# An S4 convolution gated by a feed-forward branch on Trainium2: the gate written back into PSUM, the kernel sums of two channel sets in one visit, and a new order of the projection stage

## The chip, the cores and the metric

The kernel runs on one core of a Trainium2 chip. A core has five engines that run side by side, each with its own queue of instructions which it takes in order: TensorE (PE in the profile, with its weight loads as PEld), VectorE (DVE), ScalarE (ACT), GpSimd (POOL) and SyncE (SP), which here only issues DMA transfers. They wait for one another through semaphores. The metric is the device time of one execution in microseconds (us).

## The reference, cut to what matters

```python
def _A_ref(u, A_re, A_im, B_re, B_im, C_re, C_im, log_dt, Dskip):
    dt = jnp.exp(log_dt)[:, None]
    logdA, dB = dt * (A_re + 1j * A_im), dt * (B_re + 1j * B_im)
    P = jnp.exp(logdA[:, :, None] * l[None, None, :])
    K = jnp.einsum("dn,dnl,dn->dl", Cc, P, dB).real
    ...  # y = causal convolution of u with K, by FFT
    return y + u * Dskip

def _B_ref(x, w1, b1, w2, b2):
    h = _gelu(jnp.einsum("bsd,df->bsf", x, w1) + b1)
    return jnp.einsum("bsf,fd->bsd", h, w2) + b2

x = A_u  # 1 x 2048 x 512
xn = _layernorm(x, axis=-1)
s = _A_ref(xn, ...)  # 128 states per channel
g = _silu(_B_ref(xn, ...))  # 512 -> 1792 -> 512
return x + s * g
```

## The kernel before, in words

The program has two stages. The first, here called the projection stage, does the layer norm, the two projections of branch B, and the convolution kernels K of branch A. The second does the convolution itself as a sequence of small DFT matmuls, multiplies by the gate and adds x. The change edits the first stage only.

*Projections.* The 2,048 rows are cut into four blocks of 512, the 1,792 hidden features into 14 sets of 128. Seven sets' weights are on the chip at a time, so the rows are passed twice: 8 x 7 = 56 steps of one row block and one feature set. Every fp32 operand is split into a rounded part and a rest (h and l at the end of a name), and each product is the sum of three fp32r matmuls. A step goes through five kinds of work. `first_half` (token F, in two halves of 6 matmuls, lines 243 to 252) sums into a PSUM bank with the tag `f1`; there are two such banks. `gate` (G, line 264, ScalarE) adds b1 and applies gelu, from that bank into the SBUF tile `hf`, of which there are two. `gate_high` (H, line 270, ScalarE) rounds `hf` to `hh`, and `ffn_rest` (R, line 276, VectorE) subtracts to get the rest `hl`. `second_part` (S, four pieces of 3 matmuls, lines 289 to 291) sums `hh` and `hl` times w2 into four PSUM banks `z`, over the seven sets. The row transposes of the layer norm (TF) use the `f1` banks too: ScalarE copies them out to `xh`, VectorE subtracts to `xl`.

*Convolution kernels.* The 512 channels are cut into 32 sets of 16. For a set, TensorE computes phases (A, line 593), ScalarE or VectorE rounds them (B), VectorE wraps them (C), ScalarE takes sines (N), GpSimd makes magnitudes (Z), and VectorE multiplies both into the tables e1 and e2 (E, three pieces, lines 642 to 649; two buffers of each table). `gen_sum` (Q, line 657) then sums over the states in 64 small matmuls of a 128 x 32 tile, into one PSUM bank with the tag `sm`; `gen_out` (U) copies the result out on ScalarE and `gen_keep` (UD) sends it to DRAM.

*The order.* The instructions of each engine stand in the order in which the tokens of the string `ORDER` are run; no scheduler moves them. Further tokens: P, steps of the parameters of 128 channels; W, WB and WS, loading and splitting of weights; L with a second letter, the layer norm (LS statistics, LR root, LC scaling); O and ZA to ZD, the z banks' way out. In the names that are shown later, `f_2_3` is row block 2 of the eight passes and feature set 3 of the seven; `kg` is the bank of `gen_sum`, `xT` a transpose, `ra` a set's phases, `w1l` the rest of a weight.

Of the kernel before, what the change touches and what calls it, by code (L numbers as in the profile page):

```python
# [20 lines left out]
P = 128  # L21
# [27 lines left out]
WS.0.3 LD.0 LD.1 P.0 WS.1.0 WS.1.1 P.0 P.0 WS.1.2 G.0 F.1.0 LS.2.0 W.2 LS.3.1 H.0 R.0 WB.2 S.0.0 P.0  # L49
S.0.1 LS.3.0 LL.4 WS.1.3 P.0 WS.2.0 LL.5 W.3 F.1.1 WS.2.1 WB.3 S.0.2 LS.2.1 WS.2.2 G.1 WS.2.3 W.4 S.0.3  # L50
F.2.0 P.0 F.2.1 H.1 WS.3.0 R.1 WS.3.1 P.0 S.1.0 WS.3.2 WB.4 G.2 P.0 WS.4.0 S.1.1 W.5 WS.3.3 P.0 H.2
WS.4.1 P.0 WB.5 F.3.0 P.0 S.1.2 P.0 WS.4.2 LR.2 F.3.1 G.3 S.1.3 R.2 WS.5.0 WS.5.1 KL.0.0 F.4.0 WS.4.3.1
W.6 F.4.1 LC.2 H.3 LC.3 S.2.0 G.4 KL.0.1 TF.2.0 WB.6 BB A.0.0 TH.2.0 LS.5.0 R.3 S.2.1 KL.1.0 TF.2.1
LS.4.0 B.0.0.1 TH.2.1 TL.2.0 C.0.0 WS.6.0 S.2.2 S.2.3 H.4 TF.3.0 A.0.1 KL.1.1 WS.5.2 S.3.0 LS.5.1 WS.6.1
Z.0 B.0.1 P.0 P.1 TH.3.0 S.3.1 C.0.1 S.3.2 A.1.0 N.0.0 TL.2.1 S.3.3 KL.2.0 LD.2 TL.3.0 WS.6.2 B.1.0.1
C.1.0 R.4 F.5.0 TF.3.1 Z.1 LD.3 LS.4.1 N.0.1 A.1.1 B.1.1.1 F.5.1 S.4.0 WS.5.3.1 TH.3.1.1 C.1.1 G.5 S.4.1
E.0.0 S.4.2 S.4.3 E.0.1 TL.3.1 F.6.0 H.5 N.1.0 R.5 F.6.1 LR.4 N.1.1 F.7.0 E.0.2 G.6 A.2.0 B.2.0.1 S.5.0
KL.2.1 LC.5 H.6 F.7.1 S.5.1 P.1 LC.4 C.2.0 WS.6.3 LK.0 F.8.0 S.5.2 A.2.1 G.7 KL.3.0 H.7 B.2.1 P.1 F.8.1
R.6 G.8 KL.3.1 C.2.1 N.2.0 S.5.3 F.9.0 E.1.0 N.2.1 Q.0 A.3.0 S.6.0 S.6.1 S.6.2 F.9.1 Z.2 E.1.1 R.7 U.0
E.1.2 P.1 LD.5 B.3.0.1 LD.4 C.3.0 O.0.0 TF.4.0 KL.4.0 Q.1 Z.3 O.0.1 H.8 S.6.3 TH.4.0 O.0.3 G.9 A.3.1  # L60
S.7.0 TL.4.0 B.3.1.1 P.1 H.9 S.7.1 C.3.1 O.0.2 KL.4.1 TF.4.1 UD.0 LL.6 TH.4.1 R.8 F.10.0 F.10.1 E.2.0
S.7.2 S.7.3 N.3.0 E.2.1 A.4.0 TL.4.1 P.1 S.8.0 R.9 KL.5.0 U.1 E.2.2 N.3.1 B.4.0.1 G.10 OK.0 S.8.1 F.11.0
E.3.0 F.11.1 S.8.2 C.4.0 A.4.1 S.8.3 Q.2 G.11 B.4.1 H.10 UD.1 TF.5.0 E.3.1 E.3.2 LK.1 F.12.0 H.11 TH.5.0
C.4.1 A.5.0 KL.6.0 LS.6.0 F.12.1 B.5.0.1 S.9.0 S.9.1 R.10 N.4.0 G.12 S.9.2 TL.5.0 TF.5.1 P.1 N.4.1 C.5.0
KL.5.1 S.9.3 F.13.0 A.5.1 U.2 TH.5.1 F.13.1 R.11 S.10.0 P.1 B.5.1 Z.4 P.1 P.1 Q.3 C.5.1 N.5.0 TL.5.1
S.10.1 P.1 E.4.0 P.1 UD.2 U.3 F.14.0 N.5.1 H.12 E.4.1 S.10.2 KL.6.1 UD.3 S.10.3 R.12 E.4.2 Z.5 G.13 A.6.0
S.11.0 S.11.1 F.14.1 H.13 LK.2 E.5.0 R.13 E.5.1 LL.7 S.11.2 S.11.3 B.6.0.1 C.6.0 Q.4 Z.6 S.12.0 G.14
A.6.1 KL.7.0 F.15.0 E.5.2 P.1 S.12.1 LS.7.0 B.6.1 LS.7.1 F.15.1 P.2 C.6.1 S.12.2 A.7.0 S.12.3 G.15 LS.6.1
F.16.0 B.7.0 C.7.0 LR.6 N.6.0 A.7.1 S.13.0 LC.6 KL.8.0 S.13.1 U.4 H.14 R.14 P.1 H.15 F.16.1 N.6.1 LC.7
P.2 UD.4 E.6.0 B.7.1 R.15 S.13.2 LD.6 KL.7.1 C.7.1 F.17.0 Z.7 S.13.3 F.17.1 G.16 TF.6.0 O.1.0 O.1.2 Q.5  # L70
A.8.0 E.6.1 G.17 TF.7.0 S.14.0 TH.6.0 P.2 TH.7.0 E.6.2 O.1.1 U.5 O.1.3 H.16 KL.8.1 TL.6.0 TL.7.0 B.8.0
N.7.0 Z.8 S.14.1 S.14.2 N.7.1 S.14.3 F.18.0 OK.1 UD.5 C.8.0 TF.6.1 A.8.1 P.2 Q.6 F.18.1 S.15.0 B.8.1.1
R.16 TH.6.1 S.15.1 C.8.1 S.15.2 U.6 KL.9.0 S.15.3 E.7.0 H.17 E.7.1 S.16.0 W.7 S.16.1 G.18 WB.7 A.9.0
KL.9.1 F.19.0 F.19.1 R.17 E.7.2 B.9.0 TL.6.1 N.8.0 S.16.2 W.8 LD.7 S.16.3 N.8.1 G.19 S.17.0 TF.7.1 C.9.0
A.9.1 E.8.0 P.2 H.18 KL.10.0 TH.7.1 E.8.1 Q.7 B.9.1.1 UD.6 C.9.1 KL.10.1 H.19 D S.17.1 S.17.2 A.10.0
E.8.2 S.17.3 N.9.0 WB.8 F.20.0 TL.7.1 P.2 F.20.1 U.7 KL.11.0 N.9.1 R.18 Z.9 B.10.0 S.18.0 C.10.0 E.9.0
A.10.1 Q.8 G.20 F.21.0 XL.0 W.9 S.18.1 B.10.1 C.10.1 KL.12.0 N.10.0 E.9.1 N.10.1 WB.9 S.18.2 E.9.2 R.19
S.18.3 W.10 F.21.1 A.11.0 F.22.0 U.8 B.11.0 C.11.0 S.19.0 KL.11.1 G.21 H.20 S.19.1 A.11.1 S.19.2 UD.7
Z.10 B.11.1 P.2 P.2 F.22.1 UD.8 LK.3 S.19.3 R.20 F.23.0 WB.10 G.22 C.11.1 E.10.0 N.11.0 S.20.0 Z.11
A.12.0 F.23.1 N.11.1 S.20.1 Q.9 H.21 O.2.0 S.20.2 E.10.1 E.10.2 B.12.0 KL.12.1 F.24.0 H.22 C.12.0 A.12.1  # L80
# [89 lines left out]
def kernel(  # L170
# [1036 lines left out]
```

## Time and profile before

| | before |
|---|---|
| three timed runs | 547.81, 548.02, 549.68 us; median 548.02 |
| the profiled execution | 548.29 us, span on the core 546.5 us |
| mean granted TensorE clock | 0.996 |
| projection stage, by the last large matmul | to about 407 us |
| ScalarE, busy over the span | 394.5 us (72%) |
| VectorE, busy over the span | 463.9 us (85%) |
| GpSimd, busy over the span | 279.1 us (51%) |

Busy times are sums over one execution. Matmuls overlap in the records: each row lasts about 0.4 us where the next starts after 0.235, so TensorE's progress is read from starts, not from durations. A group's row gives the line, engine, operation, tiles (out<-in), shape, count, then the busy time in us and the mean of one in ns, and behind the last bar the time that the engine stood idle ahead of these instructions and who ended it. A row of waits gives who waited for whom, the sum in us, the count and the longest.

### The profile page before, as it was taken

The numbers are of one execution on the slowest core, as the hardware profiler recorded it, in microseconds if no ns is written. First come the engines' busy times: TensorE is split into PE (matmuls) and PEld (weight loads), VectorE is DVE, ScalarE is ACT, GpSimd is POOL, SyncE is SP. The second block draws the span as 40 slices with busy tenths as digits, with TensorE's granted clock in tenths as the row PEclk, the third lists the DMA queues.
The fourth block names the chain that finished last, engine by engine and source line by source line (L and its number), as shares of the span: only waits on it lengthen the run. The fifth ranks groups of instructions, "written<-read, shape, count | busy, mean of one in ns | idle before, by whom it ended". The sixth has DMA issues, their size and how long they took to land.

```text
span 546.5 us, 16626 instructions
## 1 busy us (share of the span) xinstructions
PE 526.9 (96%) x6999; PEld 421.2 (77%) x6999; DVE 463.9 (85%) x736; ACT 394.5 (72%) x570; POOL 279.1 (51%) x385
## 2 busy tenths in 40 slices
PE   8898999999999999999999999999999999999993
PEld 7666787778776777777777777777789998997971
DVE  6899989999999889999888797789557688787896
ACT  3777998898987899959799777889664573652430
POOL 5648379358968559996854296356301001203031
PEclk9999999999999999999999999999999999999998
DMA  8937526744385172837038412913547749361562
GB/s 228 315 124 227 196 83 221 237 150 146 121 245 180 33 237 90 270 102 198 18 110 263 123 47 84 188 45 103 204 160 221 136 127 189 120 194 67 182 208 93
DMA packets 88391, 85.85 MB, mean 157 GB/s; under 512 B 42134, under 2 KB 65050, under 8 KB 87292
## 3 DMA queue, kind: packets, MB, share of 16 engines
q1 hardware_dynamic: 79248, 66.43, 41.6%
q0 software_dynamic: 8768, 17.83, 10.6%
q8 instruction: 55, 0.90, 0.7%
q10 hardware_dynamic: 300, 0.53, 0.3%
q14 instruction: 20, 0.16, 0.1%
HBM read 51.22 MB, written 33.55 MB: 155 GB/s over the span
## 4 chain that ended last, share of the span: by engine, by line
PE 76%; DVE 17%; issue 2%; ACT 1%; POOL 1%; DMA 1%; DVEq 0%; ACTq 0%; POOLq 0%
PE s L913 11%; PE z L289 8%; PE z L290 7%; PE z L291 7%; PE f L250 7%; PE f L252 7%; PE f L251 7%; PE s L891 6%; PE sa L949 6%; PE kg L657 5%; PE ph L593 2%; DVE hl L276 2%; DVE ra L607 2%; DVE e L646 1%; PE y L989 1%
## 5 line engine op out<-in xcount | busy, mean ns | idle before, releaser
L619 POOL TENSOR_TENSOR mm<-mm,rc 128x32 f32<-128x32 f32 (+4 forms) x150 | 115.4, 769 | 11.8
L289 PE MATMUL z<-w2h,hh 128*128 128x512 f32 x224 | 97.8, 437 | 0.0
L250 PE MATMUL f<-xh,w1h 128*128 128x512 f32 x220 | 91.4, 416 | 0.0
L291 PE MATMUL z<-w2h,hl 128*128 128x512 f32 x224 | 88.4, 395 | 0.3 <-DVE hl L276 0.3
L252 PE MATMUL f<-xh,w1l 128*128 128x512 f32 x220 | 87.1, 396 | 1.7 <-DVE w1l L235 1.7
L290 PE MATMUL z<-w2l,hh 128*128 128x512 f32 x224 | 88.6, 395 | 0.0
L251 PE MATMUL f<-xl,w1h 128*128 128x512 f32 x220 | 86.7, 394 | 0.0
L913 PE MATMUL s<-X,mc 64*64 64x128 f32 x1536 | 60.4, 273 | 0.2 <-issue 0.2
L930 DVE TENSOR_TENSOR t<-s,uh 128x512 f32<-128x512 f32 x64 | 41.0, 684 | 22.8 <-ACT uh L921 22.6
L276 DVE TENSOR_TENSOR hl<-hf,hh 128x512 fp32r<-128x512 f32 x56 | 52.9, 948 | 4.6 <-ACT hh L270 4.6
L616 POOL COPY mm<-rc 128x32 f32<-128x32 f32 x30 | 13.4, 446 | 77.7 <-DVE e L649 53.4
L264 ACT ACTIVATE hf<-f,b1s 128x512 f32<-128x512 f32 x56 | 38.2, 688 | 20.4 <-DVE hl L276 11.7
L252 PEld LDWEIGHTS f<-xh,w1l 128*128 128x128 f32 x220 | 41.3, 188 | 12.9 <-DVE w1l L235 3.0
L289 PEld LDWEIGHTS z<-w2h,hh 128*128 128x128 f32 x224 | 42.5, 190 | 10.5 <-issue 1.0
L291 PEld LDWEIGHTS z<-w2h,hl 128*128 128x128 f32 x224 | 42.1, 188 | 10.7 <-DVE hl L276 0.7
L607 DVE SCALAR_TENSOR_TENSOR ra<-ra,ph 128x512 f32<-128x512 f32 x64 | 43.6, 681 | 7.5 <-ACT ra L601 6.5
L913 PEld LDWEIGHTS s<-X,mc 64*64 64x64 f32 x1536 | 44.5, 133 | 5.8 <-issue 1.7
L290 PEld LDWEIGHTS z<-w2l,hh 128*128 128x128 f32 x224 | 42.3, 189 | 8.3 <-DVE w2l L235 0.2
L250 PEld LDWEIGHTS f<-xh,w1h 128*128 128x128 f32 x220 | 41.5, 189 | 9.2 <-ACT hf L264 0.2
L251 PEld LDWEIGHTS f<-xl,w1h 128*128 128x128 f32 x220 | 41.4, 188 | 9.0
L921 ACT COPY uh<-s 128x512 f32<-128x512 f32 x32 | 18.7, 586 | 38.3 <-PE s L913 18.4
L642 DVE TENSOR_TENSOR e<-mm,ra 128x1024 f32<-128x1024 f32 x32 | 42.0, 1311 | 4.7 <-POOL pr_h L524 2.4
(184 smaller groups left out, 1161.1 us busy)
## 6 DMA issues: line engine op xcount, KB each, us to landing
x<-in_A_u_dram SPq DMA_DIRECT2D x8, 512.0 KB
xs<-x SPq DMA_DIRECT2D x8, 512.0 KB
xt_h<-xh POOLq DMA_DIRECT2D x4, 1024.0 KB, 5.5
xt_l<-xl POOLq DMA_DIRECT2D x4, 1024.0 KB, 7.6
kgd<-ko SPq DMA_DIRECT2D x32, 128.0 KB
za<-zo SPq DMA_DIRECT2D x4, 1024.0 KB
xh<-xt_h POOLq DMA_DIRECT2D x4, 1024.0 KB, 6.1
xl<-xt_l POOLq DMA_DIRECT2D x4, 1024.0 KB, 10.1
```

What stands on the lines that cost most here:

```text
L250: PE.matmul(p, wh[:, k, :], xh[:, k, :], start=(k == 0), stop=False)
L251: PE.matmul(p, wh[:, k, :], xl[:, k, :], start=False, stop=False)
L252: PE.matmul(p, wl[:, k, :], xh[:, k, :], start=False, stop=(k == KD - 1))
L276: V.tensor_sub(hl, hf, hh)
L289: PE.matmul(z, hh[:, s], wh, start=(f0 == 0 and not rows), stop=False)
L290: PE.matmul(z, hh[:, s], wl, start=False, stop=False)
L291: PE.matmul(z, hl[:, s], wh, start=False, stop=(f0 == FA - 1))
L607: V.scalar_tensor_tensor(ra[:, 0, c], ra[:, 1, c], MAGIC, p, op0=ALU.subtract, op1=ALU.subtract)
L619: GP.tensor_mul(mv[:, :, 0:3:2, w:2 * w], mv[:, :, 0:3:2, 0:w], rc[:, 2 + 2 * i:4 + 2 * i, :].rearrange("p j c -> p c j").unsqueeze(3).to_ ...
L642: V.tensor_mul(e1, m1.unsqueeze(1).to_broadcast([P, 2, CH, N1]), ra[:, :, :, :N1])
L913: PE.matmul(p[ka * 64:(ka + 1) * 64, r, o, :, jj], w, xf[b][h, c, :, k, :], start=(c == 0), stop=(c == 1), skip_group_check=True)
L930: V.tensor_mul(t, p[:, i, :, 1].unsqueeze(1).to_broadcast([P, 2, 2, P]), uh)
```

## The change

Three things are edited.

1. `gate` writes its result back into the PSUM bank that it reads; `hf` is no tile of its own any more. `gate_high` and `ffn_rest` therefore read the bank, and it is free for new matmuls only when `ffn_rest` has run. `hh` and `hl` get four buffers instead of three.
2. `gen_sum` runs for every second set, over the tables of two neighbouring sets: 128 matmuls into one bank of twice the used width. `gen_out` and `gen_keep` run half as often, on twice the size.
3. `ORDER` is replaced. Besides the places, it says for which halves ScalarE and for which VectorE rounds the phases: VectorE has 31 of the 64 in place of 35.

```diff
 ORDER = """
-WS.0.3 LD.0 LD.1 P.0 WS.1.0 WS.1.1 P.0 P.0 WS.1.2 G.0 F.1.0 LS.2.0 W.2 LS.3.1 H.0 R.0 WB.2 S.0.0 P.0
...
+WS.0.3 P.0 LD.0 P.0 P.0 WS.1.0 WS.1.1 WS.1.2 F.1.0 G.0 H.0 LD.1 W.2 R.0 WS.1.3 F.1.1 WS.2.0 LS.2.0 G.1
...
     def gate(v, f):
-        hf = wka.tile([P, TB * P], F32, tag="hf", name=f"hf_{v}_{f}", bufs=2)
-        A.activation(hf, pt.pop((v, f)), AF.Gelu_apprx_tanh, bias=b1s[:, f:f + 1])
+        hf = pt.pop((v, f))
+        A.activation(hf, hf, AF.Gelu_apprx_tanh, bias=b1s[:, f:f + 1])
         ht[v, f] = hf

     def gate_high(v, f):
         hf = ht[v, f]
-        hh = wka.tile([P, TB * P], F32R, tag="hh", name=f"hh_{v}_{f}", bufs=3)
+        hh = wka.tile([P, TB * P], F32R, tag="hh", name=f"hh_{v}_{f}", bufs=4)
         A.copy(hh, hf)
         ht[v, f] = (hf, hh)

     def ffn_rest(v, f):
         hf, hh = ht[v, f]
-        hl = wka.tile([P, TB * P], F32R, tag="hl", name=f"hl_{v}_{f}", bufs=3)
+        hl = wka.tile([P, TB * P], F32R, tag="hl", name=f"hl_{v}_{f}", bufs=4)
         V.tensor_sub(hl, hf, hh)
         ht[v, f] = (hh, hl)
...
     def gen_sum(s):
-        e1, e2 = gen[s]["e"]
-        p = pss.tile([P, DD, N2], F32, tag="sm", name=f"kg{s}")
-        for d in range(DD):
-            for c in range(2):
-                for g in range(G):
-                    PE.matmul(p[g * N1:(g + 1) * N1, d, :], e1[:, c, g * DD + d, :], e2[:, c, g * DD + d, :],
-                              start=(c == 0), stop=(c == 1), skip_group_check=True)
+        p = pss.tile([P, 2, DD, N2], F32, tag="sm", name=f"kg{s}")
+        for n in range(2):
+            e1, e2 = gen[s - 1 + n]["e"]
+            for d in range(DD):
+                for c in range(2):
+                    for g in range(G):
+                        PE.matmul(p[g * N1:(g + 1) * N1, n, d, :], e1[:, c, g * DD + d, :], e2[:, c, g * DD + d, :],
+                                  start=(c == 0), stop=(c == 1), skip_group_check=True)
         gen[s]["p"] = p

     def gen_out(s):
-        gen[s]["ko"] = ko = par.tile([P, DD, N2], F32, tag="ko", name=f"ko{s}", bufs=2)
+        gen[s]["ko"] = ko = par.tile([P, 2, DD, N2], F32, tag="ko", name=f"ko{s}")
         A.copy(ko, gen[s]["p"])

     def gen_keep(s):
-        b, j = divmod(s, SPB)
-        SY.dma_start(kgd[b][:, j * DD * N2:(j + 1) * DD * N2], gen.pop(s)["ko"].rearrange("p a b -> p (a b)"))
+        b, j = divmod(s // 2, SPB // 2)
+        SY.dma_start(kgd[b][:, j * 2 * DD * N2:(j + 1) * 2 * DD * N2], gen.pop(s)["ko"].rearrange("p n a b -> p (n a b)"))
```

The three places of which the prediction speaks, as the engines' queues have them. First, TensorE at the sums of the first sets (`e_0` and `e_1` are the tables of sets 0 and 1); before:

```order
L252 MATMUL f_1_2_895<-xh_600,w1l_408 128x512
L657 MATMUL kg_907<-e_0_764,e_0_763 32x64 x32
L593 LDWEIGHTS lh_869
L593 MATMUL ph_0_940<-cbs,lh_869 128x512
L289 MATMUL z_0_373<-w2h_640,hh_6_828 128x512
```

and now:

```order
L287 MATMUL z_0_929<-w2h_250,hh_0_860 128x512
L288 MATMUL z_0_929<-w2l_251,hh_0_860 128x512
L289 MATMUL z_0_929<-w2h_250,hl_0_894 128x512
L359 MATMUL xT_0_939<-ident,x_406 128x128 x4
L655 MATMUL kg_962<-e_0_756,e_0_755 32x64 x32
L655 MATMUL kg_962<-e_1_855,e_1_854 32x64 x32
L287 MATMUL z_1_930<-w2h_250,hh_0_860 128x512
```

The sums of set 0 wait for those of set 1 and stand with them. Second, VectorE ahead of the first new transposes, some 35 to 45 us into the span (`x_228` holds the rows that are transposed, `al` and `rec` are copies of parameters); now:

```order
L562 COPY al_502<-pT_504 128x128
L562 COPY rec_501<-pT_504 128x8x16
L274 TENSOR_TENSOR hl_2_514<-f_0_2_432,hh_2_512 128x512
L233 TENSOR_TENSOR w2l_452<-w2s_454,w2h_451 128x512
L233 TENSOR_TENSOR w1l_519<-w1s_456,w1h_518 128x512
L328 TENSOR_SCALAR va_531<-mv_374,eps 128x4
```

and, behind the root's small operations:

```order
L343 TENSOR_SCALAR x_228<-x_228,mv_374,rs_375 128x512 x4
L274 TENSOR_TENSOR hl_3_604<-f_0_3_464,hh_3_516 128x512
L318 BN_STATS bst_0_635<-x_445 128x6
L319 BN_AGGR mv_633<-bst_0_635 128x2
L274 TENSOR_TENSOR hl_4_638<-f_0_4_578,hh_4_602 128x512
L374 TENSOR_TENSOR xl_607<-xT_0_608,xh_606 128x4x128
```

Before, `hl_2` stood between the root and the scaling of `x_228`, the weight rest w2l of set 3 ahead of the copies, and w1l of set 3 and `hl_1` further ahead still. The transposes behind (xT_0_608 and the next) take the banks that `hl_3` and `hl_4` read. Third, two sets of block 2 and the transposes behind them; TensorE now:

```order
L250 MATMUL f_2_3_1620<-xh_937,w1l_450 128x512
L286 MATMUL z_0_1667<-b2r,ones 128x512
L287 MATMUL z_0_1667<-w2h_250,hh_0_1476 128x512
L288 MATMUL z_0_1667<-w2l_251,hh_0_1476 128x512
L289 MATMUL z_0_1667<-w2h_250,hl_0_1519 128x512
L287 MATMUL z_1_1668<-w2h_250,hh_0_1476 128x512
L288 MATMUL z_1_1668<-w2l_251,hh_0_1476 128x512
L289 MATMUL z_1_1668<-w2h_250,hl_0_1519 128x512
L286 MATMUL z_2_1669<-b2r,ones 128x512
```

and, after three more of z_2 and a phase matmul, `xT_0_1707` and `xT_0_1713`. VectorE's queue at that place:

```order
L343 TENSOR_SCALAR x_1163<-x_1163,mv_1345,rs_1346 128x512 x2
L343 TENSOR_SCALAR x_1301<-x_1301,mv_1345,rs_1346 128x512 x2
L639 TENSOR_TENSOR e_6_1659<-mm_1433,ra_1441 128x1024
L643 TENSOR_TENSOR e_6_1660<-mm_1433,ra_1441 128x32x32
L645 TENSOR_TENSOR e_6_1660<-mm_1433,ra_1441 128x16x32
L646 SCALAR_TENSOR_TENSOR e_6_1660<-mm_1433,ra_1441 128x16x32
L605 SCALAR_TENSOR_TENSOR ra_1523<-ra_1523,ph_1_1603 128x512
L391 TENSOR_TENSOR zo_1665<-z_1_930,b2b 128x4x128
L274 TENSOR_TENSOR hl_2_1694<-f_2_2_1606,hh_2_1684 128x512
L274 TENSOR_TENSOR hl_3_1696<-f_2_3_1620,hh_3_1691 128x512
```

The two rests that free both banks stand behind a scaling and a whole set of table multiplies; the tables of set 6 can be written only when the visit of sets 4 and 5 has passed on TensorE.

More of the change, by code (lines that the diff above doesn't have):

```diff
@@ L54 @@
[L54 to L68, printed above, removed]
```

146 lines of the change are left out of this document (79 added, 67 removed).

## The prediction

> **What bounds the kernel now.** I read the engine totals and the granted clock first, then the busy time by stretch (stretch, engine busy time with instruction counts, clock, DMA share and GB/s), then TensorE's waits.
>
> ```profile
> span 546.5 us, 16626 instructions
> PE 526.9 (96%) x6999; PEld 421.2 (77%) x6999; DVE 463.9 (85%) x736; ACT 394.5 (72%) x570; POOL 279.1 (51%) x385
> ...
> 0.00:60.00 60.00, 52.44 (x256) 41.35 (x257) 52.91 (x126) 41.20 (x68) 33.88 (x74) 1.00 0.73 228
> 60.00:160.00 100.00, 100.00 (x979) 77.90 (x978) 94.22 (x146) 89.94 (x126) 72.77 (x101) 1.00 0.51 162
> 160.00:260.00 100.00, 98.07 (x949) 74.83 (x948) 91.99 (x117) 84.94 (x123) 76.14 (x86) 1.00 0.55 166
> 260.00:400.00 140.00, 140.00 (x1471) 108.04 (x1471) 112.17 (x151) 112.01 (x141) 75.30 (x102) 1.00 0.45 120
> ```
>
> ```profile
> PE ph L593 <- DVE ra L607: 2.2, 4, 0.9
> PE xT L361 <- DVE xl L376: 1.8, 1, 1.8
> PE f L252 <- DVE w1l L235: 1.7, 2, 1.5
> ...
> PE xT L361 <- ACT hf L264: 0.9, 2, 0.6
> ...
> PE z L291 <- DVE hl L276: 0.3, 1, 0.3
> ```
>
> TensorE sets the time. From 60 to 400 us it stands idle for 1.93 us in all (the 98.07 of 100), at the full clock. VectorE is behind it by little: 94 and 92 of 100 in the first two stretches. So a saving on VectorE or ScalarE moves the end only where it ends a TensorE wait, and those lie nearly all in the first 60 us (7.6 us idle, part of it the start). The large prize that is left is TensorE's own work. The stage after 400 us is not edited; I carry it over.
>
> The profiled execution took 548.29 us: its span of 546.5 and 1.8 around it. That is 0.3 above the median of 548.02, so I sum against 548.3.
>
> **Part 1: sums of two sets in one visit.** The matmuls stay 2,048; the visits fall from 32 to 16. TensorE's timeline around one visit (start, duration), and the groups:
>
> ```profile
> 99.20 0.40 PE L289 MATMUL z<-w2h,hh 128*128 128x512 f32 x1
> 99.43 0.40 PE L290 MATMUL z<-w2l,hh 128*128 128x512 f32 x1
> 99.67 0.39 PE L291 MATMUL z<-w2h,hl 128*128 128x512 f32 x1
> 99.98 1.10 PE L657 MATMUL kg<-e,e 128*32 128x64 f32 x64
> 101.01 0.50 PE L289 MATMUL z<-w2h,hh 128*128 128x512 f32 x1
> 101.35 0.40 PE L290 MATMUL z<-w2l,hh 128*128 128x512 f32 x1
> ```
>
> ```profile
> L657 PE MATMUL kg<-e,e 128*32 128x64 f32 x2048 | 35.2, 220 | 0.0
> L657 PEld LDWEIGHTS kg<-e,e 128*32 128x32 f32 x2048 | 30.1, 110 | 10.5 <-issue 8.6 <-ACT ra L630 0.7 <-ACT ra L627 0.4
> ```
>
> Large matmuls start 0.235 us apart (99.20 to 99.67 is two slots). From 99.67 to 101.35 there are two slots (0.47) and the visit, which so costs 1.68 - 0.47 = 1.21 us. Its 64 weight loads take 30.1 / 32 = 0.94. A second set that follows at once should add about those 0.94, so a pair saves 0.27, and 16 pairs **4.3 us**. From below: if the second adds its whole 35.2 / 32 = 1.10, 0.11 x 16 = 1.8 us. From above: without the last load's 0.11 it adds 0.83, and 16 pairs save 6.1. This term rests on no wait going away.
>
> The copies out fall from 32 to 16 and the transfers of 128 KB to 16 of 256 KB; both lie beside TensorE. What it adds is a wait: both sets' tables (two buffers each) are held until the visit, so VectorE's next table multiply, and behind it the rests, wraps and scalings in its queue, waits for TensorE to pass the visit. Before, one set's multiplies fitted in between. Counted in the new order with durations of the groups, TensorE has more work up to the end of a visit than VectorE has between the two multiplies in 10 of the 15 places: some 29 us in sum, 8 to 10 of them after each of sets 11 and 21. This is paid from VectorE's idle time: 5.8 + 8.0 + 27.8 us in the three stretches above, and what part 2 frees. I cost it at nothing; with that cover gone it shows up as the third rival.
>
> **Part 2: the gate stays in PSUM.** The groups (what they write and read, shape, count, busy time and mean ns of one, idle before):
>
> ```profile
> L276 DVE TENSOR_TENSOR hl<-hf,hh 128x512 fp32r<-128x512 f32 x56 | 52.9, 948 | 4.6 <-ACT hh L270 4.6
> L376 DVE TENSOR_TENSOR xl<-xT,xh 128x512 fp32r<-128x512 f32 x16 | 10.5, 678 | 0.0
> L264 ACT ACTIVATE hf<-f,b1s 128x512 f32<-128x512 f32 x56 | 38.2, 688 | 20.4 <-DVE hl L276 11.7 <-PE f L252 6.4 <-PE f L260 1.5
> L264 ACT ACT_TABLE_LOAD x29 | 37.2, 1283 | 1.6 <-DVE hl L276 1.1
> L270 ACT CAST hh<-hf 128x512 fp32r<-128x512 f32 x56 | 34.2, 617 | 1.7 <-PE z L290 1.4
> L370 ACT CAST xh<-xT 128x512 fp32r<-128x512 f32 x15 | 8.5, 584 | 5.4 <-PE xT L361 5.4
> L663 ACT COPY ko<-kg 128x256 f32<-128x256 f32 x32 | 11.6, 361 | 4.8 <-PE kg L657 4.6
> L921 ACT COPY uh<-s 128x512 f32<-128x512 f32 x32 | 18.7, 586 | 38.3 <-PE s L913 18.4 <-issue 10.2 <-ACT Z L960 7.3
> ```
>
> The rest hl now reads PSUM and SBUF, as xl does: 678 instead of 948 ns, 56 x 0.27 = 15.1 us off VectorE. Four fewer rounds there (35 to 31; 0.685 each) make it 17.8. [...]
>
> ScalarE: the cast hh reads PSUM as xh does (-33 ns x 56 = -1.8); 16 copies of the L921 size replace 32 (9.4 for 11.6: -2.2); the two orders hold 66 and 60 table loads (-7.7); four more rounds (+2.7). That is -9.0 us. No row has ScalarE writing PSUM. From below I take the copy of this size (586 ns: -5.7 us), from above a read and a write one after the other (1,376 ns: +38.5); I take 688, since the function, shape and source are those of L264.
>
> On the clock all this is worth nothing by itself. What it costs is **the bank**: it was free for new matmuls when the gate had run, and is now held through gate, cast and rest: 0.69 + 0.58 + 0.68, against 0.69. There are two such banks. In the new order the TensorE work between the filling of a bank and its next use has about the same median as before (7.3 against 7.0 us, at 0.235 a slot), so mostly it covers the longer hold.
>
> **Part 3: the order.** What it can win is the early waits. TensorE's and VectorE's rows:
>
> ```profile
> 19.32 0.50 PE L252 MATMUL f<-xh,w1l 128*128 128x512 f32 x1 [1.52 <-DVE w1l L235]
> ...
> 38.81 0.63 PE L361 MATMUL xT<-ident,x 128*128 128x128 f32 x4 [0.28 <-ACT hf L264]
> ...
> 40.92 0.66 PE L361 MATMUL xT<-ident,x 128*128 128x128 f32 x4 [0.57 <-ACT hf L264]
> 41.33 0.48 PE L289 MATMUL z<-w2h,hh 128*128 128x512 f32 x1
> ...
> 44.75 0.66 PE L361 MATMUL xT<-ident,x 128*128 128x128 f32 x4 [1.77 <-DVE xl L376]
> ...
> 49.02 0.39 PE L250 MATMUL f<-xh,w1h 128*128 128x512 f32 x1
> ```
>
> ```profile
> 34.50 0.68 DVE L235 TENSOR_TENSOR w1l<-w1s,w1h 128x512 fp32r<-128x512 f32 x1
> ...
> 36.94 0.95 DVE L276 TENSOR_TENSOR hl<-hf,hh 128x512 fp32r<-128x512 f32 x1
> ...
> 37.81 3.79 DVE L345 TENSOR_SCALAR x<-x,mv,rs 128x512 f32<-128x512 f32 x4
> ```
>
> The 1.52 us at 19.32 stay: the same vector steps stand ahead of that rest. Behind it the new order has 84 large matmuls and two transposes up to the first new transposes: 19.7 + 0.2, so TensorE is there at 39.2. Their bank is free after the rest of set 3. VectorE: the copies that ended at 34.50 now have three subtractions fewer ahead of them (0.6 each from start to start): 32.7; then hl of set 2 and two weight rests: 34.5; the root, 2.44 from 34.50 to 36.94 less a weight rest of 0.6: 36.3; the four scalings, 3.7: 40.0; the rest: 40.8. TensorE waits 1.6 us. From there to the first matmul of set 5 it has 9 matmuls, three visits of transposes at 0.5 (0.41 to the next matmul at 41.33, which then runs late) and two phase matmuls at 0.2: 4.0 us, and the rests that free the next banks come in time by the same count (42.3 for the second). Set 5 starts at 44.8, short of three matmuls and a phase matmul done before (0.9): at 45.7 it stands where it stood at 49.02. That is 3.3 us won; I take **3.0**. From above: with the wait of 1.6 gone too, 4.9. From below: if the scalings and both rests behind them come 3 us later still, it is won back entirely: 0.
>
> Later than 60 us, 1.9 us of idle time can go and new waits on banks can come. No row shows these; from both sides they are bounded by -1.9 and by the second rival's +16. I take +1.5, nearer to the low end, since before 60 us is the only stretch where such waits show, although the old order too had some twenty banks with hardly more TensorE work than ScalarE and VectorE work ahead of their release.
>
> **Sum:** 548.3 - 4.3 - 3.0 + 1.5 = **542.5 us**. Its own range, by the bounds of the parts near it: 538 to 546.
>
> **The rivals.**
> *Won and given back (no change).* The first term stands, but early waits only move to the next bank and the later order waits as much as it wins: 548.3 - 4.3 + 3.5 = 547.5. For it: VectorE at 94 of 100 has to follow TensorE. Against it: it gets 17.8 us lighter.
>
> *The held bank (slower).* The place: TensorE fills two banks with sets 2 and 3 of the third block of rows and has only z matmuls and a phase left before it needs both again for transposes, while VectorE has a root, four scalings, a whole table set and two more ahead of the two rests.
>
> ```profile
> L642 DVE TENSOR_TENSOR e<-mm,ra 128x1024 f32<-128x1024 f32 x32 | 42.0, 1311 | 4.7 <-POOL pr_h L524 2.4 <-ACT ra L630 2.3
> ...
> L646 DVE TENSOR_TENSOR e<-mm,ra 128x1024 f32<-128x1024 f32 x32 | 45.2, 1412 | 0.0
> ...
> L649 DVE SCALAR_TENSOR_TENSOR e<-mm,ra 128x512 f32<-128x512 f32 x32 | 28.9, 904 | 0.0
> L648 DVE TENSOR_TENSOR e<-mm,ra 128x512 f32<-128x512 f32 x32 | 25.9, 809 | 0.0
> ```
>
> VectorE: 1.8 for the root, 3.8 for the scalings, 4.4 for the table set and three at 0.68, 12 us. TensorE from the end of set 2: 12 + 8 + 1 matmuls, 4.9 us. If VectorE begins that list only when set 2 is filled, TensorE waits 7 us. Three more such places, counted in the order the same way (block 1 sets 0 to 2, block 3 sets 1 to 3, the last block's sets 3 to 5), are worth 3.3, 2.1 and 3.1: together 16, which puts the time at 548.3 - 7.3 + 16 = 557. It decides as soon as these waits pass 7.3 us. For it: rests stood behind gates and delayed ScalarE for 11.7 us before (L264's last column). Against it: VectorE can do the root and scalings before the visit ahead of its table set, and then reaches both rests in 7 us or so after that visit, while TensorE needs about 8. [...]
>
> *The doubled hold-up (slower).* ScalarE's gate into its own bank takes the upper bound, 1.38: in the stretch with 89.94 busy it gains 10, and ScalarE is full: some 10 us of waits, 551 to 555. Against it: nothing in the trace; for it: no row excludes it.
>
> *VectorE starves behind the visits.* The 29 us of part 1 fall where VectorE has no idle time, and TensorE waits for rests: half of it would give 548.3 - 7.3 + 10 = 551. Against it: from 60 to 260 us these add to some 15, beside 13.8 idle and 9 freed.
>
> **How the numbers follow.** A change of 0.5% (2.7 us) is about what a measurement of this kernel tells from none. Forecast 0.58, and 0.03 for a larger gain with all bounds on its side (537); no change 0.15; the held bank 0.14; the slow gate 0.05; the starving VectorE 0.05. So faster 0.61, same 0.15, slower 0.24. The range runs from 537, the forecast with the early term at its bound and no new waits, to 553, which takes in the starving VectorE and leaves out the upper part of the other slow cases.
>
> **What would show it.** Visits: 16 groups of 128 in TensorE's timeline, about 2.15 us from the matmul ahead to the second behind, less two slots; TensorE's start-to-start time over the stage shorter by 4 us. PSUM: hl near 680 ns, hh near 585, the gate near 690. Order: set 5 starting near 45 us, and fewer than 6 us idle on TensorE before 60. The forecast is wrong if TensorE's waits name hl before f or xT for more than 4 us after 60, if the gate takes over 0.9 us, or if ScalarE or VectorE shows over 97 of 100 in a stretch where TensorE idles.

## The result and the profile after

| | before | after |
|---|---|---|
| median of the timed runs | 548.46 us (4 runs) | 541.06 us (4 runs, 539.74 to 542.16) |
| the profiled execution | 548.29 us, span 546.5 | 539.74 us, span 537.9 |
| last large matmul of the projection stage starts | 407.00 us | 395.56 us |
| from there to TensorE's end | 131.0 us | 134.0 us |

The ratio is 0.9861, 95% interval 0.9827 to 0.9895: the change makes the kernel 1.4% faster, 7.6 us of 548.5. The forecast was 542.5. In the two profiled executions the first stage gains 11.4 us and the second gives 3.0 back; that is 1 us more than the medians show, because the profiled execution of the changed kernel is the fastest of its four.

Engine totals and stretches of the changed kernel (stretch, then busy time and instruction counts of each engine, clock, DMA share, GB/s):

```profile
span 537.9 us, 16530 instructions
...
PE 518.8 (96%) x6999; PEld 421.7 (78%) x6999; DVE 432.8 (80%) x732; ACT 388.6 (72%) x552; POOL 258.8 (48%) x384
```

```profile
0.00:60.00 60.00, 55.96 (x274) 45.23 (x275) 52.13 (x130) 43.20 (x71) 32.56 (x73) 1.00 0.75 228
60.00:160.00 100.00, 100.00 (x1046) 79.15 (x1045) 93.83 (x155) 89.57 (x124) 71.37 (x104) 1.00 0.44 144
160.00:260.00 100.00, 98.03 (x900) 76.68 (x899) 80.57 (x114) 84.03 (x117) 72.08 (x97) 1.00 0.61 185
260.00:400.00 140.00, 140.00 (x1617) 111.41 (x1619) 99.61 (x148) 113.79 (x143) 63.97 (x92) 1.00 0.47 133
```

TensorE is 3.5 us busier before 60 us than it was. From 60 to 400 us it idles 1.97 us, as before (1.93). VectorE has fallen from 92 to 81 of 100 in the third stretch, and by 31.1 us over the span (463.9 to 432.8), where the prediction had 17.8: the rests give the 15.1 that were foreseen (52.9 to 37.8), and two pieces of the table multiplies another 6.7 (54.8 to 48.1 in sum) that were not. GpSimd fell by 20.3 (279.1 to 258.8), which was not foreseen either; ScalarE by 5.9 (394.5 to 388.6), where the prediction had 9.0. TensorE's waits, the five that speak to the prediction:

```profile
PE s L911 <- ACT uh L919: 3.0, 1, 3.0
PE f L250 <- DVE w1l L233: 1.5, 1, 1.5
...
PE f L250 <- issue: 1.3, 1, 1.3
...
PE ph L591 <- DVE ra L605: 0.4, 2, 0.2
...
PE f L248 <- DVE hl L274: 0.2, 1, 0.2
```

The waits for xT are gone. The rest hl, which would be named here if the held banks cost much, holds TensorE up once, for 0.2 us. The largest wait is new and lies in the second stage.

A pair visit on TensorE's timeline, and its group:

```profile
154.63 0.39 PE L289 MATMUL z<-w2h,hl 128*128 128x512 f32 x1
154.95 2.00 PE L655 MATMUL kg<-e,e 128*32 128x64 f32 x128
156.87 0.50 PE L287 MATMUL z<-w2h,hh 128*128 128x512 f32 x1
157.21 0.40 PE L288 MATMUL z<-w2l,hh 128*128 128x512 f32 x1
```

```profile
L655 PE MATMUL kg<-e,e 128*32 128x64 f32 x2048 | 31.9, 220 | 0.0
```

From 154.63 to 157.21 are 2.58 us. Less two slots, 0.47, the visit costs 2.11. The same reading of the 14 visits that stand alone in the trace of before gives 1.22 each, so a pair saves 0.33, and 16 pairs 5.3 us. The operations around the gate:

```profile
L274 DVE TENSOR_TENSOR hl<-f,hh 128x512 fp32r<-128x512 f32 x56 | 37.8, 682 | 10.5 <-ACT hh L268 10.5
...
L262 ACT ACTIVATE f<-f,b1s 128x512 f32<-128x512 f32 x56 | 37.2, 665 | 19.5 <-PE f L250 18.2 <-PE f L258 0.4 <-DVE ra L605 0.2
L268 ACT CAST hh<-f 128x512 fp32r<-128x512 f32 x56 | 32.4, 587 | 2.2 <-PE z L288 1.2
```

The gate into its own bank takes 665 ns, a little less than the 688 into SBUF before. The rest of idle time ahead of the gates now ends with TensorE (18.2), where 11.7 us had ended with hl. The early stretch, first on TensorE, then on VectorE:

```profile
39.06 0.40 PE L289 MATMUL z<-w2h,hl 128*128 128x512 f32 x1
39.60 0.66 PE L359 MATMUL xT<-ident,x 128*128 128x128 f32 x4
...
43.59 0.40 PE L248 MATMUL f<-xh,w1h 128*128 128x512 f32 x1
```

```profile
36.38 2.57 DVE L343 TENSOR_SCALAR x<-x,mv,rs 128x512 f32<-128x512 f32 x4
38.87 0.68 DVE L274 TENSOR_TENSOR hl<-f,hh 128x512 fp32r<-128x512 f32 x1
```

The scalings start where the prediction put them (36.3) but take 2.57 us instead of 3.7, and hl ends at 39.55, so the wait of 1.6 us at the new transposes is not there.

The start of the second stage: ScalarE, VectorE and TensorE wait in a chain for the stores of zi to gd.

```profile
397.85 2.25 POOL L442 DMA_DIRECT2D gd<-zi  x4 [19.67 <-ACT zi L433]
...
403.31 0.58 ACT L919 COPY uh<-s 128x512 f32<-128x512 f32 x1 [3.25 <-DMA gd<-zi]
403.34 1.29 DVE L928 TENSOR_TENSOR t<-s,uh 128x512 f32<-128x512 f32 x2 [6.45 <-DMA gd<-zi]
...
404.73 0.67 PE L911 MATMUL s<-X,mc 64*64 64x128 f32 x16 [2.97 <-ACT uh L919]
```

uh and t need nothing that these stores bring. What they have in common is a place. In the built program (the addresses are read from it, no profile shows them) zi lies at byte 92448 of each partition before the change and at 104736 after: b2st and one (2 KB each) had used the ring of hf, and now the first tiles of the rings hh and hl (four each, 16 KB) are laid out ahead of zi, 12 KB more than hf's 4 KB. At 104736 the 8 KB of zi overlap a buffer of uh (from 104416) and of t (from 106464). So uh and t must not be written before the stores have read zi.

### The profile page after: what moved, and what is told of

The parts are those of the page before. It is cut to its first block, busy times and chain, and to the rows that moved or that the text cites. A ratio compares the mean times of both kernels' runs of the same rounds, so it can differ in the third digit from the quotient of the medians.

```text
span 537.9 us, 16530 instructions
## 1 busy us (share of the span) xinstructions
PE 518.8 (96%) x6999; PEld 421.7 (78%) x6999; DVE 432.8 (80%) x732; ACT 388.6 (72%) x552; POOL 258.8 (48%) x384
## 4 chain that ended last, share of the span: by engine, by line
PE 82%; DVE 7%; POOL 3%; ACT 3%; issue 2%; DMA 2%; POOLq 0%; DVEq 0%; ACTq 0%
PE s L911 11%; PE z L287 9%; PE z L289 8%; PE z L288 8%; PE f L248 8%; PE f L250 8%; PE f L249 8%; PE s L889 6%; PE sa L947 6%; PE kg L655 5%; PE ph L591 2%; PE y L987 1%; DMA w1s<-in_B_w_dram 1%; DMA gd<-zi 1%; DVE hl L274 1%
## 5 line engine op out<-in xcount | busy, mean ns | idle before, releaser
L616 POOL TENSOR_TENSOR mm<-mm,rc 128x32 f32<-128x32 f32 (+4 forms) x150 | 97.6, 651 | 11.8
L287 PE MATMUL z<-w2h,hh 128*128 128x512 f32 x224 | 95.6, 427 | 0.0
L262 ACT ACTIVATE f<-f,b1s 128x512 f32<-128x512 f32 x56 | 37.2, 665 | 19.5 <-PE f L250 18.2
L613 POOL COPY mm<-rc 128x32 f32<-128x32 f32 x30 | 14.5, 485 | 70.5 <-DVE e L646 39.9
L274 DVE TENSOR_TENSOR hl<-f,hh 128x512 fp32r<-128x512 f32 x56 | 37.8, 682 | 10.5 <-ACT hh L268 10.5
```

Source lines behind the costliest of these rows:

```text
L274: V.tensor_sub(hl, hf, hh)
L287: PE.matmul(z, hh[:, s], wh, start=(f0 == 0 and not rows), stop=False)
L616: GP.tensor_mul(mv[:, :, 0:3:2, w:2 * w], mv[:, :, 0:3:2, 0:w], rc[:, 2 + 2 * i:4 + 2 * i, :].rearrange("p j c -> p c j").unsqueeze(3).to_ ...
```

## The experiments

Times are given against the runs of the kernel before on the same chip, as a ratio with its 95% interval; a step of 0.001 is 0.55 us.

### The place of zi

In the changed kernel, zi is allocated earlier:

```diff
-        if n == 2:
-            ln["zi"] = wka.tile([P, TB, D], F32, tag="zi", name="x23")
...
         stage_second(0)
+        ln["zi"] = wka.tile([P, TB, D], F32, tag="zi", name="x23")
         bias_load()
```

> The changed kernel with one edit: the tile zi (8 KB in each partition, the last normalised group that is stored to gd at the end of the first stage) is allocated ahead of the bias rows instead of with the third group, so that it lies at 88352 to 96544 and no longer under the second stage's uh and t tiles. Theory (the second stage's first copies uh and t wait until the four stores gd<-zi have read zi, because they overwrite its place, and this is the 3 us that the second stage gives back): the 2.97 us wait of TensorE for uh at 404.7 us is gone, the second stage is back at about 131 us, the time falls by 2.5 to 3 us to about 538. Rival (the second stage starts 11 us earlier and the stores or its loads are simply late; place of the tile plays no part): the wait stays, under 0.5 us of difference.

Measured: 537.38 us, ratio 0.9795 (0.9778 to 0.9811), 3.7 us faster than the changed kernel. ScalarE and VectorE at the same point, which now wait for their products alone:

```profile
402.51 0.59 ACT L918 COPY uh<-s 128x512 f32<-128x512 f32 x1 [1.76 <-PE s L910]
...
403.12 1.29 DVE L927 TENSOR_TENSOR t<-s,uh 128x512 f32<-128x512 f32 x2 [1.27 <-ACT uh L918]
```

The last large matmul starts at 396.24, and the second stage takes 131.8 us from there. The counterpart on the kernel before:

```diff
         stage_second(0)
+        for m in ("hh", "hl"):
+            V.memset(wka.tile([P, TB * P], F32R, tag=m, name=f"{m}_0", bufs=3)[:, :1].bitcast(F32), 0.0)
         bias_load()
```

> The kernel before with one edit: six small memsets take the places of the hh and hl tiles ahead of the bias rows, so that zi moves by 12,288 bytes to 104736, where it lies in the changed kernel, under the second stage's uh and t tiles. Nothing else differs. Theory (the place of zi alone makes the second stage wait for the stores of zi): slower than before by about 3 us, 551, with a wait of TensorE for uh of about 3 us at the start of the second stage. Rival (it was the earlier start of the second stage): within 0.5 us of before.

Measured: 552.46 us, 1.008 (1.0053 to 1.0107), 4 us slower. The second stage takes 137.9 us instead of 131.0, the first is 1.2 us shorter. The wait of TensorE, and ScalarE's row:

```profile
PE s L915 <- ACT uh L923: 4.0, 1, 4.0
```

```profile
414.61 0.58 ACT L923 COPY uh<-s 128x512 f32<-128x512 f32 x1 [4.27 <-DMA gd<-zi]
```

Both ways round, the wait comes and goes with the place of zi, and the row names the stores of zi as what ends it. Each edit moves other tiles too, but the rest of the 14 traces agrees: the six kernels that have zi at byte 104736 show a wait of TensorE for uh here, of 2.7 to 4.0 us, and the eight that have it elsewhere show none. That theory stands. The wait may not be the whole price: in the pages of five of those six the granted clock falls behind it, in one slice of some 14 us, to 8 tenths (7 in one of them), where 9 stands in the changed kernel's and in the other eight. The three other runs of the changed kernel were granted 0.987 to 0.993 in the mean, against 0.995 in the profiled one; whether that is why the runs give 3.7 us for a wait of 3.0 was not shown.

### The visits

```diff
-Q.1
+Q.0 S.7.0 ... Q.1
...
-        for n in range(2):
-            e1, e2 = gen[s - 1 + n]["e"]
+        n = s % 2
+        for e1, e2 in (gen[s]["e"],):
```

> The changed kernel with the visits to the sums undone: each pair visit is two visits of one set, with at least one second matmul group of the pass between them; the bank, the copies out and the stores stay one for a pair, the rest of the order stays. Theory (a visit costs a fixed 0.33 us beside its 64 matmuls, so that 32 visits of 1.22 us cost 39 us and 16 of 2.11 us 34 us): slower than the changed kernel by 4 to 5.5 us, about 545.5. Rival (the saving comes from fewer waits, not from the visit itself): under 1 us slower.

Measured: 548.32 us, 1.0003 (0.9985 to 1.0022), 7.8 us slower than the changed kernel, more than either had it. The group's row and two of TensorE's waits:

```profile
L658 PE MATMUL kg<-e,e 128*32 128x64 f32 x2048 | 35.2, 220 | 1.2 <-ACT ko L663 1.2
```

```profile
PE ph L592 <- DVE ra L606: 1.9, 4, 0.6
...
PE kg L658 <- ACT ko L663: 1.2, 1, 1.2
```

The group is that of before again (35.2 us, 220 ns each); at the 1.22 us read there, the single visits cost 5.3 us more in all. Some 2.7 us more are waits: for the phases, 1.5 above the changed kernel, and once for the copy out of the shared bank, which this way of undoing brings with it. Next, the pair visits alone, in the old kernel:

```diff
-Q.4 ... U.4 ... UD.4 E.6.0 ... Q.5 ... U.5
+Q.5 E.6.0 ... U.5
```

The bodies of the visit, the copy and the store are those of the change.

> The kernel before with the pair visits alone: gate in SBUF and old order, but the sums of two neighbouring sets in one visit, one copy out and one store for a pair; seven visits stand ahead of the next tables' first step where the old place of the odd set's sums was later. Theory (the visit itself is cheaper by 0.33 us for each set pair): faster than before by 4 to 5.5 us, about 543.5, less 1 to 2 us where a visit moved ahead must wait for its tables. Rival (the pair visit needs the new order to be worth anything, since it stands on its tables' last step): within 1.5 us of before.

Measured: 559.13 us, 1.0207 (1.0172 to 1.0242): 11 us slower than before, against both. What VectorE and then TensorE waited for:

```profile
DVE e L639 <- PE kg L655: 17.7, 9, 5.2
```

```profile
PE ph L591 <- DVE ra L605: 10.9, 11, 3.2
```

In the old order VectorE stands for 17.7 us ahead of a table multiply until TensorE has passed the pair's visit. The rounds and wraps in its queue come late, and TensorE loses 10.9 us at the phases. This is the prediction's rival of VectorE starving behind the visits. It is real; the new order leaves 1.1 us of it on VectorE.

### The gate in PSUM

First try:

```diff
-        hf = pt.pop((v, f))
-        A.activation(hf, hf, AF.Gelu_apprx_tanh, bias=b1s[:, f:f + 1])
+        hf = wka.tile([P, TB * P], F32R, tag="hl", name=f"hl_{v}_{f}", bufs=4)
+        A.activation(hf, pt.pop((v, f)), AF.Gelu_apprx_tanh, bias=b1s[:, f:f + 1])
...
-        V.tensor_sub(hl, hf, hh)
+        V.tensor_sub(hf, hf.bitcast(F32), hh)
```

> The changed kernel with the gate in PSUM undone: the gate writes into the SBUF tile that later holds the low part, the high part is copied from there, the subtraction runs in place on SBUF, so that the PSUM bank is free when the gate has ended; order and visits stay. The gate's output is rounded here to the matmul's type, so the low part is zero: that part of the result is left out, no instruction is. Theory (the subtraction was shortened from 948 to 682 ns by one operand in PSUM, 15 us of VectorE, and with it part of TensorE's waits went): slower by 1 to 3 us, 542 to 544. Rival one (only the order took the waits away): within 0.5 us. Rival two (holding the bank costs): faster by 1 us or more.

Measured: 554.87 us, 1.011 (1.0078 to 1.0142), 13.7 us slower than the changed kernel, beyond all three. ScalarE's row shows that the experiment was not clean:

```profile
ACT hl L262 <- PE z L288: 11.1, 6, 3.9
```

The gate now takes its tile of hl itself, where before only the rest took it, later, and ScalarE stands 11.1 us until TensorE has read an old one. The granted clock also was 0.97 in the mean before 60 us and 0.99 from 260 to 400, where the changed kernel's is 1.00 in both. With both other parts undone on top:

> The changed kernel with the pair visits and the gate in PSUM both undone, so that of the change the order alone is left (and the place of zi). As in the run with the gate alone undone, the gate's output is rounded to the matmul's type and the low part is zero: that part of the result is left out, no instruction is. Theory (the new order takes its lead for granted: VectorE must be some 17 us lighter, or TensorE waits for it at the phases): slower than the kernel before, 556 to 562. Rival (the order took the waits away by itself): 545 to 548, which is the changed kernel with 5 us for the visits.

Measured: 561.4 us, 1.0252 (1.0211 to 1.0293). It has the same flaw, so it says nothing about the order. The price of VectorE's time was then measured by itself:

```diff
-        V.tensor_sub(hl, hf, hh)
+        for a, b in ((0, 170), (170, 341), (341, 512)):
+            V.tensor_sub(hl[:, a:b], hf[:, a:b], hh[:, a:b])
```

> The changed kernel, the gate still in PSUM, with VectorE made heavier: each of the 56 subtractions is made in three pieces of 170 or 171 columns, which adds two fixed costs to each, by estimate 0.25 to 0.3 us, 14 to 17 us in all, as much as the subtraction from SBUF did. Theory (the 14 us by which the kernel with the gate in SBUF is slower come from VectorE's time): slower than the changed kernel by 8 us or more, 549 to 556, and TensorE waits for ra at the phases again. Rival (they came from the low part's tile being taken a step earlier, at the gate): within 2 us, 541 to 543.

Measured: 543.58 us, 0.9896 (0.9853 to 0.9939); the last large matmul starts at 398.84. The group and a wait:

```profile
L275 DVE TENSOR_TENSOR hl<-f,hh 128x170 fp32r<-128x170 f32 x168 | 45.0, 326 | 11.4 <-ACT hh L268 11.4
```

```profile
PE ph L592 <- DVE ra L606: 1.7, 3, 0.8
...
PE xT L360 <- DVE hl L275: 1.5, 1, 1.5
```

By their durations three pieces of 326 ns take 0.30 us more than one subtraction of 682, the upper end of the estimate. But the pieces overlap in the records (168 of them are 54.8 us in sum and 45.0 together), so VectorE got only 8.0 us heavier (440.8 against 432.8). The theory's 8 us did not come: by the ratios the loss is 1.9 us, and the two intervals overlap. The first stage of the profiled execution, the slowest of four, is 3.3 us longer. So 8.0 us of VectorE cost between nothing that can be told and 3.3 us, and one of its waits is for the held bank, at a transpose. The clean undoing has hf's two tiles back, in the place of the two bias tiles (the bias of the second product is left out of the result), and zi early:

```diff
-        hf = pt.pop((v, f))
-        A.activation(hf, hf, AF.Gelu_apprx_tanh, bias=b1s[:, f:f + 1])
+        hf = wka.tile([P, TB * P], F32, tag="hf", name=f"hf_{v}_{f}", bufs=2)
+        A.activation(hf, pt.pop((v, f)), AF.Gelu_apprx_tanh, bias=b1s[:, f:f + 1])
...
-    b2r = wka.tile([P, D], F32R, name="b2r")
...
-    b2b = wka.tile([P, D], F32, name="b2b")
```

> The changed kernel with zi ahead of the bias rows (as in the first run) and the gate in PSUM undone once more, now with its own two SBUF tiles as before the change, so that no tile is taken a step early; the place for them comes from the two bias tiles. The bias of the second product is left out of the result for that (its row matmuls read a weight tile, its copies out add a tile of ones), three small instructions and one 256 KB load of it are missing. To be compared with the first run, 537.4 us. Theory (VectorE's time has a price: 8.0 us more of it cost 2.5 us in the run with three pieces, so about 17 us more cost 5): 541 to 544. Rival one (the 14 us of the first try are the gate's own): 549 to 552. Rival two (the bank held longer costs as much as the lighter VectorE brings): 537 to 538.

Measured: 545.32 us, 0.9932 (0.9905 to 0.9959): 7.5 us slower than with zi early alone, between the theory and its first rival. Totals, the rows of hl and hh, and two of TensorE's waits:

```profile
PE 520.4 (96%) x6999; PEld 421.0 (77%) x6999; DVE 450.2 (83%) x731; ACT 391.2 (72%) x551; POOL 274.8 (51%) x384
```

```profile
L274 DVE TENSOR_TENSOR hl<-hf,hh 128x512 fp32r<-128x512 f32 x56 | 51.1, 920 | 9.8 <-ACT hh L268 9.8
...
L268 ACT CAST hh<-hf 128x512 fp32r<-128x512 f32 x56 | 34.3, 621 | 1.0
```

```profile
PE ph L589 <- DVE ra L603: 3.3, 6, 1.2
PE f L248 <- ACT hf L262: 1.7, 1, 1.7
```

So the gate in PSUM is worth 7.5 us here, and about 6 of the first try's 13.7 were its own. VectorE is 18.7 us heavier than with zi early (431.5), and the last large matmul starts at 403.25 instead of 396.24: 7.0 us, 0.38 for each of VectorE's. By the starts, the steps from a large matmul to a phase take 16.9 us in sum instead of 12.6, so 4.3 of the 7.0 are lost there, where TensorE's rows name VectorE's work on the phases. The wait for the gate, 1.7, is another matter: the chain behind it leads over a load of w2s to GpSimd's rest w2l, whose four take 1,630 ns in the mean instead of 1,408. GpSimd is 15.5 us heavier in this kernel, ScalarE 2.5. So VectorE's time carries most of the loss, and how much of it is GpSimd's was not separated.

### The order alone

The clean version, with the visits split as well:

> The same, with the pair visits undone as well, so that the new order is all that is left of the change (and the bias is left out as there). To be compared with the kernel before, 548.5 us. Theory (visits 5 us, VectorE 5 us on top of 537.4): 547 to 549, so the new order by itself is worth nothing. Rival one (the order by itself takes the early waits away): 542 to 544. Rival two (the order by itself does harm, as the first try at it had it): 555 or more.

Measured: 552.52 us, 1.0057 (1.0037 to 1.0077), between the theory and the second rival: 3.1 us slower than before. TensorE's waits:

```profile
PE ph L590 <- DVE ra L604: 5.7, 8, 1.4
...
PE kg L656 <- ACT ko L661: 1.5, 1, 1.5
```

1.5 us of this are the shared bank of the split visits, not the order. The early win is there all the same. Set 5 starts at

```profile
44.69 0.40 PE L249 MATMUL f<-xh,w1h 128*128 128x512 f32 x1
```

and, less the 0.9 that the prediction reckons as done before, stands at 45.6 where it stood at 49.02: 3.4 us. It is lost again behind: TensorE reaches the phases before VectorE has freed their bank, for 5.7 us instead of 2.2. So the new order by itself keeps nothing of its win and costs up to 3 us in all.

### VectorE lighter

In the kernel before, and then in the changed kernel with zi early:

```diff
-        V.tensor_mul(e2[:, 1, :, H:], m2[:, :, H:], ra[:, 1, :, up])
-        V.scalar_tensor_tensor(e2[:, 0, :, H:], m2[:, :, H:], -1.0, ra[:, 0, :, up], op0=ALU.mult, op1=ALU.mult)
+        V.tensor_mul(e2[:, :, :, H:], m2[:, :, H:].unsqueeze(1).to_broadcast([P, 2, CH, H]), ra[:, :, :, up])
```

> The kernel before with VectorE made lighter at another place: the second half of the tables e2 is made in one operation instead of two, without the factor -1 for one component, so the sign of a quarter of that table is left out of the result. By the rows of before (809 and 904 ns against 1412 ns for the same size in one) VectorE is 0.3 us lighter per set, 9.6 us in all; gate, order and visits stay. Theory (VectorE's lateness is what TensorE waits for in the old kernel as well): faster than before by 2 to 5 us. Rival (the old kernel's waits are set by its order, TensorE is full otherwise): within 1 us of before.

Measured: 547.21 us, 0.9981 (0.9966 to 0.9996). VectorE is 10.5 us lighter (453.4) and the time 1.0 us shorter. That is at the rival's bound; in the old order, lighter tables buy little, 0.1 us for one of VectorE's.

> The changed kernel with zi ahead of the bias rows, and VectorE lighter in the way already tried on the kernel before: the second half of e2 in one operation, without the factor -1, so the sign of a quarter of that table is left out of the result. By the rows (742 and 758 ns against 1322 ns) VectorE is about 6 us lighter. To be compared with zi alone, ratio 0.9795 to the kernel before. Theory (TensorE is full now, with about 3 us of waits left before the second stage, so VectorE costs where it is late and brings nothing where it is not): within 0.6 us, ratio 0.978 to 0.9805. Rival (VectorE's time has the same price in both directions, 0.4 us for one): 2.4 us faster, ratio 0.975.

Measured: 537.15 us, 0.9771 (0.9755 to 0.9787), against 0.9795 (0.9778 to 0.9811) without the edit. The intervals overlap, and the ratio lies between the theory and the rival. VectorE became only 2.2 us lighter (429.3), though the rows of these pieces fall from 48.1 to 40.7 us. In the changed kernel's trace the records of the two operations overlap by 78 ns in each set, 2.5 us in sum; the rest of the difference was not traced. This run settles nothing.

### One more wait

```diff
-WS.0.3 P.0 LD.0 P.0 P.0 WS.1.0 WS.1.1 WS.1.2 F.1.0
+WS.0.3 P.0 LD.0 WS.1.0 WS.1.1 P.0 WS.1.2 P.0 F.1.0
```

> The changed kernel with zi ahead of the bias rows and one more edit of the order: the rest of the second weight tile, w1l of slot 1, stands on VectorE ahead of two steps of the parameters. Theory (the 1.5 us wait of TensorE for w1l at 19.5 us is VectorE's order alone): 1 to 1.5 us faster than with zi alone, about 536. Rival (the parameters then come late for the first phases, and the wait goes there): within 0.5 us of 537.4.

Measured: 537.76 us, 0.9798 (0.9774 to 0.9822), no difference to zi early alone. The early rows on TensorE:

```profile
23.46 0.50 PE L250 MATMUL f<-xh,w1l 128*128 128x512 f32 x1 [0.44 <-DVE w1l L233]
26.81 0.50 PE L248 MATMUL f<-xh,w1h 128*128 128x512 f32 x1 [0.76 <-ACT w1h L231]
```

The wait of 1.5 us is gone, and waits of 0.44 and 0.76 stand at the next two weights. The first is VectorE's again, which does statistics of the layer norm ahead of that rest; the second follows its load, for which ScalarE's w1h waited 1.67 us.

## Why the prediction was right in the sum, and where it was not

The time, 541.06, lies 1.4 us below the forecast. The steps, in the prediction's order:

- **Visits.** Foreseen -4.3, measured -5.3 by the timeline, within the bounds. That the second set costs less behind the first held; the size was off because it adds 0.89 us, not 0.94. The wait of VectorE for the visit, costed at nothing, is 1.1 us on VectorE, and TensorE's waits for the phases fell to 0.4. By the runs the visits are worth more, 6.9 to 7.8, since splitting them also brings waits.
- **"On the clock all this is worth nothing by itself."** This step on the gate in PSUM failed. It is worth 7.5 us in the new order. VectorE's time was taken as covered because VectorE idles some of the time; undoing its 18.7 us cost TensorE 7.0, most of it at the phases. The price is not one number: 10.5 us lighter in the old order gained 1.0, and 8.0 heavier in the new one lost 1.9 by the ratios, which overlap.
- **The order.** Foreseen -3.0 from early waits and +1.5 from later ones. In the changed kernel the early win is larger: set 5 starts at 43.59 and, less the 0.9 done before, stands at 44.5 where it stood at 49.02, so 4.5. The term's step was the scalings: 3.7 foreseen, 2.57 measured. Of waits on banks 0.2 us came. With the order alone the early win is 3.4, near the forecast; the term that was too small is the later one, +1.5, where some 6.5 are lost behind set 5 (1.5 of it the shared bank). In the finished kernel, with VectorE lighter, they are not there.
- **"The stage after 400 us is not edited; I carry it over."** This step failed: 3.0 us in the profiles and 3.6 by the runs, shown both ways by the place of zi. No row of the profile before could tell it; the allocations of the two programs could.

Going from the kernel before to the changed one by the runs, in steps of the ratio: the order with split visits +0.0057, pair visits -0.0125, the gate in PSUM -0.0137, the place of zi +0.0066. They sum to -0.0139, 7.6 us. (The sum is closed because the runs form a chain; that each size stands for its part alone holds only in this sequence, and the first step also has the closer matmuls of the last section, about 1.8 us by their starts.) That the sum came within 1.4 us is in part luck: the visits and the early win were right in kind, while the later loss of the order (1.5 foreseen, 6.5 in the run of the order alone), the gate's gain (nothing foreseen, 7.5) and the loss behind 400 us (nothing foreseen, 3.6) came out against one another.

Of the rivals, the held bank and the slow gate did not come: hl holds TensorE for 0.2 us, and the gate takes 665 ns. The held bank is not far off, though: with VectorE 8.0 us heavier it held up a transpose for 1.5. The rival of the starving VectorE came only in the old order, and its sum in the prediction does not follow: half of 29 us is 14.5, not 10, which gives 555.5. With the bank kept through gate, cast and rest the kernel is the faster one, by 7.5 us against the clean undoing.

The fastest kernel of all is the changed one with zi early: 537.4 us, 0.9795 of before (0.9778 to 0.9811), below the changed kernel's interval.

## What to carry to other kernels

The parts of this change to a tuned schedule did not add: the pair visits gain 5 to 8 us in the new order and lose 11 in the old one, so undo such parts one at a time within the finished change, and look whether the undoing itself brings a wait. VectorE, behind the bounding engine at 80 to 95 of 100, still had a price, 0.1 us for one in the old order and up to 0.4 in the new one; it was not one number, and has to be measured in the order that is used. When a ring of tiles changes its size, compare the addresses of what is allocated behind it: a tile of another stage may now lie under one that is still being stored, which here was a wait of 3.0 us.

## What was not expected of the hardware

The subtraction's duration goes with where its inputs lie: 682 ns in the mean with one in PSUM, 920 with both in SBUF. The rows by tile (least, median and greatest duration in ns) of the changed kernel, and then of the one with the gate back in SBUF:

```profile
L274 DVE TENSOR_TENSOR hl<-f,hh x56: 658/682/692, 19.4 to 380.4; 128x512 fp32r<-128x512 f32 x56
```

```profile
L274 DVE TENSOR_TENSOR hl<-hf,hh x56: 668/793/1621, 18.6 to 388.1; 128x512 fp32r<-128x512 f32 x56
```

The least is nearly the same; with both inputs in SBUF the greatest is more than twice as long. The long ones stand beside GpSimd's work: the 10 of these 56 that have no GpSimd instruction beside them take 680 to 692 ns, the other 46 take 971 in the mean. In the kernel before, also with both in SBUF, the 14 that have no tensor operation of GpSimd beside them take 679 to 693 ns, the other 42 take 1,036 in the mean. With one input in PSUM none takes over 692, such an operation beside it or not (43 with, 13 without). GpSimd's products, in the same two kernels but with zi early in the first, take 649 ns against 710 in the mean:

```profile
L614 POOL TENSOR_TENSOR mm<-mm,rc 128x32 f32<-128x32 f32 (+4 forms) x150 | 97.4, 649 | 11.8
```

```profile
L614 POOL TENSOR_TENSOR mm<-mm,rc 128x32 f32<-128x32 f32 (+4 forms) x150 | 106.6, 710 | 11.8
```

So, with both inputs in SBUF, the subtractions beside GpSimd's work are longer, and GpSimd's products are longer in the mean. No run here took GpSimd's work away, so the cause was not shown.

Large matmuls that follow one another start 232.9 ns apart in the mean before and 231.5 after, over some 1,200 of them about 1.8 us. The whole difference is in the z matmuls, which read hh and hl: 233.0 before, 229.4 after. Those of f have 232.8 and 233.4. It goes with the places of the tiles: in the three kernels that have hh and hl from byte 133696 on, the z matmuls are 233.0 to 233.1 apart, in the eleven that have them between 88352 and 112928 it is 229.3 to 230.1. The kernel before with zi moved is one of these, at 230.1 with its old order, gate and visits. So it comes with the layout, which the change of the rings brought along; why the place matters stays open.
